# Issuing the first weight load ahead of SyncE's part in the entry barrier of a decode kernel

## The chip, the cores and the metric

The kernel runs on one core of one Trainium2 chip. The time is device microseconds of one execution, the median over several runs. A program can also run in a slower state. The "span" of a profile is counted from the first instruction that the trace shows (here SyncE's first one) to the last; the time is about 1.3 us longer than the span (654.95 and 653.6 in one run of the kernel before).

## The reference, cut to what matters

One decode step for two sequences: layer norm, grouped-query attention over a long cache, and a small gated MLP beside it.

```python
B, Sq, D = 2, 1, 512
Hq, Hkv, Sk, Dh = 32, 8, 32768, 128        # bf16 everywhere
xn = layernorm(x)
q  = xn @ wq                                # wq: 512 x 4096
p  = softmax(q @ k_cache^T * Dh**-0.5)      # k_cache: 2 x 8 x 32768 x 128
s  = (p @ v_cache) @ wo                     # wo: 4096 x 512
g  = silu(mlp(xn))                          # w3: 512 x 1792, w4: 1792 x 512
out = x + s * g
```

There are 16 (sequence, KV head) groups, each with 8 MiB of K and 8 MiB of V. Everything that has to be read comes to 280.5 MB; the output is 2 KB. The MLP's first branch (w1, w2) vanishes for a sequence of length one, and the kernel does not read it.

## The kernel before

The kernel has a static plan: SyncE issues nearly all loads on one DMA queue, in order, and waits only where a buffer has to come free first. The first load, wq, is recorded inside the framework's block; all other instructions are recorded after that block is closed.

```python
wq_t = kbuf[:, 2 * SLOT:3 * SLOT]
s_wq, s_out = nc.alloc_semaphore("s_wq"), nc.alloc_semaphore("s_out")
first = sp.dma_start(out=wq_t[:, 0:DK * HD], in_=A_wq.rearrange("(p k) f -> p (k f)", k=DK))
first.then_inc(s_wq, 16)
tc.no_tile_sem_insts.add(first.ins.name)

tc.close()
tc.compile()
# ... (semaphores)
k_w3 = d_w3.after(sp.dma_start(out=w34[:, 0:W4O], in_=...B_w3...), 16)
k_w4 = d_w4.after(sp.dma_start(out=w34[:, W4O:W4O + FK * D], in_=...B_w4...), 16)
# ... 
load_k(0)                                    # 8 MiB
load_half(A_v_cache, vbuf[:, :], s_v, 0, 1)  # 4 MiB

k_x0 = V(dve.memset(x_bf[:, :], 0.0))        # VectorE; then ScalarE loads x
wait(act, k_x0)
k_x = d_x.after(act.dma_start(out=x_bf[0:QP:BS, :], in_=A_x...), 16)
# ... layer norms, q = xn @ wq, the MLP: "the prologue" below
wait(sp, k_h2)
load_half(A_v_cache, vbuf[:, :], s_v, 0, 0)  # the first V group's other half, over w3 and w4
for m in range(1, NG):
    sp.wait_ge(p_k, m)                       # half of K group m-1 is used
    load_k(m)
    sp.wait_ge(p_o, m)                       # V group m-1 is used
    load_v(m)
# ... wo in seven parts, then the end:
k = V(dve.tensor_tensor(out=sg, in0=s_ps, in1=g4, op=ALU.mult))
k = V(dve.tensor_tensor(out=out4, in0=sg, in1=x4, op=ALU.add))
wait(sp, k)
sp.dma_start(out=out[:, 0, :].rearrange("b (n c) -> n b c", c=QW), in_=out4[0:QP:BS, :]).then_inc(s_out, 16)
sp.wait_ge(s_out, 16)
```

What the source does not show is how the built program starts. There is an entry block, in which every engine arrives at a barrier (GpSimd gathers the others, after it has set a few constants) and jumps. Then comes the framework's block, whose only work is the wq load, and which ends in another jump. Then come two more barriers, and only then the kernel's other instructions.

The softmax here doesn't subtract the row's maximum and nothing guards it: scores larger than these inputs give would overflow.

Of the kernel before, what the change touches and what calls it, by code (L numbers as in the profile page):

```python
# [43 lines left out]
def take(eng, sem, n=1):  # L44

    eng.wait_ge(sem, n).then_inc(sem, -n)  # L46


@with_exitstack
def kernel(  # L50
# [14 lines left out]
    nc = tc.nc  # L65
# [99 lines left out]
    first = sp.dma_start(out=wq_t[:, 0:DK * HD], in_=A_wq.rearrange("(p k) f -> p (k f)", k=DK))  # L165
# [2 lines left out]

    tc.close()
    tc.compile()  # L170

    d_x, d_w3, d_w4 = (Count(nc, n) for n in ("d_x", "d_w3", "d_w4"))
    s_k = [nc.alloc_semaphore(f"s_k{i}") for i in range(NPART)]
# [177 lines left out]
    for t in range(NQB):  # L351
        for k in range(DK):
            for n in range(NQ):
                c = (t * NQ + n) * GW
                i = pe.matmul(
                    sc[t][32 * n:32 * n + 32, :], lhsT=xT[:, k, :],
                    rhs=wq3[:, k, c:c + GW].rearrange("p (h w e) -> p h e w", h=rep * NB, e=2),
                    start=(k == 0), stop=(k == DK - 1), tile_position=(0, 32 * n),
                )
# [32 lines left out]
    for k in range(DK):  # L392
        for n in range(NQ):
            i = pe.matmul(
                h_ps[32 * n:32 * n + 32, 0:HW], lhsT=xT[:, DK + k, :], rhs=w3v[:, k, n * HW:(n + 1) * HW],
                start=(k == 0), stop=(k == DK - 1), tile_position=(0, 32 * n),
            )
# [29 lines left out]
    for f in range(FK):  # L427
        i = pe.matmul(h2[0:32, :], lhsT=h_bf[:, f, :], rhs=w4v[:, f, :], start=(f == 0), stop=(f == FK - 1))  # L428
# [27 lines left out]
    with act.Fori(0, NG) as m:  # L456
        for j in range(4):
            c = (NR - 1) * rep + 32 * j
            i = act.copy(  # L459
                out=z[32 * j:32 * j + 32, :, :, c:c + rep],  # L460
                in_=qr[32 * j:32 * j + 32, :, :, bass.ds(m * rep, rep)],
            )
        i.then_inc(s_z, 1)
        for i in range(NPART):
            take(act, s_sc)
            act.activation(  # L466
                out=eps_[i][:, :], in_=sc[i][:, :], func=ACT.Exp, scale=inv_sqrt_dh, accum_out=rss[i][:, :]
            ).then_inc(s_e, 1)
        take(act, s_o)
        act.copy(out=ob[:, :], in_=o[:, :]).then_inc(s_ob, 1)  # L470
# [4 lines left out]
    def then(inst):  # L475
        inst.then_inc(s_d, 1)
        take(dve, s_d)
# [52 lines left out]
    for j in range(NQ):  # L530
        n = B * NS if j < NQ - 1 else B * NS - 1
# [144 lines left out]
```

## Time and profile before

| | before |
|---|---|
| time, median of 6 runs | 654.96 us (654.88 to 655.34) |
| span of the profiled run | 654.2 us |
| share of the span that SyncE's queue filled | 99.2% of 16 DMA engines |
| TensorE, VectorE, ScalarE busy | 60%, 53%, 12% |
| wq issued, its first packet | 0.74 us, 1.76 us |
| last wo part landed | 651.47 us |

The page's slices of the kernel before, 40 equal ones over the span: the busy share of the 16 DMA engines in tenths and the bytes moved in GB/s. Below them is the first row of the table of DMA queues (queue, kind: packets, MB, share).

```profile
DMA  8999999999999999999999999999999999999997
GB/s 368 442 439 448 442 413 429 445 445 429 417 445 445 441 401 445 445 437 405 445 445 445 409 437 445 445 433 409 445 445 445 397 445 445 445 425 417 437 429 293
...
q1 hardware_dynamic: 6492, 280.50, 99.2%
```

Queue q1 is SyncE's. The DMA engines are full from the second slice to the last but one. A packet of 32768 B takes 1.213 us in the trace, which makes 16 x 32768 B / 1.213 us = 432 GB/s. Most of the bytes (243 MB) come in packets of 65536 B, which take 2.418 us each, or 434 GB/s on 16 engines. The scatter of the slices (397 to 448) I do not take for a changing rate: a packet is counted whole in the slice in which it starts, one slice of 16.4 us holds 6.8 rounds of 16 such packets, and counting 6 or 7 of them gives 385 or 449.

The start in time, the timeline of the kernel before (start us, duration us, engine, line, operation, out<-in; in brackets the idle time before it and what ended that). SPq is SyncE's own sequence, where the duration of a DMA is that of its issue only.

```profile
0.74 0.40 SPq L165 DMA_DIRECT2D kbuf<-in_A_wq_dram  x1
1.91 0.33 SPq L202 DMA_DIRECT2D vbuf<-in_B_w_dram  x1
1.92 0.20 POOL L238 MEMSET ident<- 128x128 bf16 x1 [1.47 <-POOLq L170]
2.04 0.27 DVE L230 MEMSET x_bf<- 128x256 uint32 x1 [2.04 <-PEq L170]
```

And who waited for whom at the start, the view of waits of SyncE's queue (total us, times, longest us), its last two rows:

```profile
SPq L660 <- PEq L660: 0.7, 1, 0.7
SPq L170 <- PEq L170: 0.4, 2, 0.3
```

SyncE has nothing to do in the entry block. It stands at the barrier for 0.7 us before the first byte of 280 MB has even been asked for. (The barrier is released by GpSimd, whose gather runs at 0.53 us; the view names the engine whose signal came last by the profile.)

The end, the chain of waits of the kernel before, its last rows (start us, duration us, what):

```profile
614.73 36.74 DMA kbuf<-in_A_wo_dram
651.47 0.04 issue
651.52 0.26 PE bank L614 x4
651.78 0.02 issue
651.80 0.30 DVE sg L638
652.10 0.02 issue
652.13 0.29 DVE out L640
```

The last wo part stood 36.74 us in the queue, then there are 0.26 us of matmuls, two VectorE operations and the store. Between the two ends, the trace shows how much was in the queue each time SyncE issued another load (bytes issued before, less the bytes of packets that had ended): never less than 3.1 MB, about 7 us of work. So the time is the start of the first packet, plus one unbroken stream, plus a tail.

### The profile page before, as it was taken

Reading aid. Unit: us, or ns where it says so; the run is one execution under the profiler, and the core shown is the slowest. Engines: PE = TensorE matmul, PEld = TensorE weight load, DVE = VectorE, ACT = ScalarE, POOL = GpSimd, SP = SyncE. Lnnn points to the kernel's source line nnn. Section 1 sums busy time; section 2 is a strip of 40 time slices with the busy share of each in tenths; the row PEclk is TensorE's granted clock in tenths of the full one; section 3 lists DMA queues with packets and bytes.
Section 4 is the critical chain, followed back from the end, with each engine's and each line's share of the span. In section 5 each row is a group of like instructions: output and inputs, shape, how many; then the busy total and the mean of one; then the engine's idle time right before and its main releaser. Section 6 shows DMA issues by size and latency. Waiting matters only on the chain. (4 is left out here: it accounts for less than half of the span.)

```text
span 654.2 us, 6541 instructions
## 1 busy us (share of the span) xinstructions
PE 390.2 (60%) x2406; PEld 156.8 (24%) x2438; DVE 345.7 (53%) x412; ACT 76.6 (12%) x184; POOL 7.7 (1%) x29
## 2 busy tenths in 40 slices
PE   0648285582838648293773829367283945828785
PEld 0222132230313212131231213123121322312322
DVE  4257092653909356291844719174480926539570
ACT  1320102010010200101020010201001020010100
POOL 3100000000000000000000000000000000000000
PEclk9769788696978868698786978878697896869798
DMA  8999999999999999999999999999999999999997
GB/s 368 442 439 448 442 413 429 445 445 429 417 445 445 441 401 445 445 437 405 445 445 445 409 437 445 445 433 409 445 445 445 397 445 445 445 425 417 437 429 293
DMA packets 6508, 280.56 MB, mean 429 GB/s; under 512 B 736, under 2 KB 1000, under 8 KB 1256
## 3 DMA queue, kind: packets, MB, share of 16 engines
q1 hardware_dynamic: 6492, 280.50, 99.2%
q8 instruction: 2, 0.03, 0.0%
q14 instruction: 2, 0.02, 0.0%
q10 hardware_dynamic: 12, 0.01, 0.0%
HBM read 280.50 MB, written 0.00 MB: 429 GB/s over the span
## 5 line engine op out<-in xcount | busy, mean ns | idle before, releaser
L562 PE MATMUL bank<-T,z 128*128 128x512 bf16 x992 | 271.6, 418 | 187.2 <-PEq L46 181.7
L489 DVE STREAM_TRANSPOSE T<-kbuf 128x1024 int32<-128x1024 int32 x256 | 290.5, 1206 | 127.2 <-DVEq L46 127.2
L562 PEld LDWEIGHTS bank<-T,z 128*128 128x128 bf16 x1024 | 96.0, 103 | 350.2 <-issue 274.4
L579 PE MATMUL bank<-vbuf,pt 128*16 128x512 bf16 x1024 | 75.6, 461 | 2.5 <-PEq L46 2.5
L466 ACT ACTIVATE ep<-bank 128x512 bf16<-128x512 f32 x32 | 19.1, 597 | 436.1 <-ACTq L46 436.1
L510 DVE RECIPROCAL rec<-bank 128x1 f32<-128x1 f32 (+1 forms) x17 | 2.9, 169 | 122.7 <-DVEq L46 122.7
L579 PEld LDWEIGHTS bank<-vbuf,pt 128*16 128x16 bf16 x1024 | 28.0, 104 | 41.9 <-issue 25.1
L498 DVE STREAM_TRANSPOSE pt<-ep 128x512 bf16<-128x512 bf16 x32 | 22.7, 708 | 22.0 <-DVEq L46 22.0
L544 PE MATMUL bank<-ob,sel_o 128*128 128x128 f32 x136 | 20.6, 298 | 16.4 <-PEq L46 16.4
L572 PE MATMUL bank<-ones_f,sm 128*128 128x1 f32 x32 | 6.6, 277 | 31.3 <-PEq L46 31.3
L544 PEld LDWEIGHTS bank<-ob,sel_o 128*128 128x128 f32 x136 | 17.7, 204 | 21.8 <-issue 21.8
L470 ACT COPY ob<-bank 128x512 f32<-128x512 f32 x16 | 9.4, 586 | 105.7 <-ACTq L46 105.7
L459 ACT ACT_TABLE_LOAD x16 | 20.5, 1283 | 0.3
L572 PEld LDWEIGHTS bank<-ones_f,sm 128*128 128x128 f32 x32 | 5.8, 225 | 32.2 <-issue 32.2
L459 ACT COPY z<-qr 32x16 bf16 x64 | 12.9, 201 | 0.7
L428 PE MATMUL bank<-vbuf,h_bf 128*32 128x512 bf16 x14 | 5.3, 565 | 5.7 <-DVE h_bf L425 5.7
L539 PE MATMUL bank<-ident 128*1 128x1 bf16 x64 | 8.4, 165 | 0.0
L305 PE MATMUL bank<-ident,xn_bf 17*128 17x17 bf16 x4 | 0.3, 179 | 13.4 <-POOL x L296 13.4
L539 PEld LDWEIGHTS bank<-ident 128*1 128x1 bf16 x64 | 4.0, 82 | 16.2 <-issue 14.4
L518 DVE TENSOR_REDUCE oA<-xm 128x128 f32 x16 | 5.9, 366 | 3.8 <-DVEq L46 3.8
L512 DVE SCALAR_TENSOR_TENSOR xm<-bank,rec,mask 128x128 f32<-128x128 f32 (+1 forms) x17 | 6.0, 351 | 2.5 <-DVEq L46 0.2
L466 ACT ACTIVATION_READ_ACCUMULATOR ep<-bank 128x1 f32 x32 | 6.4, 199 | 0.2
(75 smaller groups left out, 55.4 us busy)
## 6 DMA issues: line engine op xcount, KB each, us to landing
vbuf<-in_A_v_cache_dram SPq DMA_DIRECT2D x4, 4096.0 KB, 29.6
kbuf<-in_A_k_cache_dram SPq DMA_DIRECT2D x2, 4096.0 KB, 22.9
kbuf<-in_A_wq_dram SPq DMA_DIRECT2D x1, 4096.0 KB, 12.5
vbuf<-in_B_w_dram SPq DMA_DIRECT2D x2, 1792.0 KB, 17.4
kbuf<-in_A_wo_dram SPq DMA_DIRECT2D x3, 1024.0 KB, 34.4
kbuf<-in_A_wo_dram SPq DMA_DIRECT2D x1, 512.0 KB, 37.1
kbuf<-in_A_wo_dram SPq DMA_DIRECT2D x1, 256.0 KB, 37.3
kbuf<-in_A_wo_dram SPq DMA_DIRECT2D x2, 128.0 KB, 36.8
```

Source lines behind the costliest of these rows:

```text
L459: i = act.copy(out=z[32 * j:32 * j + 32, :, :, c:c + rep], in_=qr[32 * j:32 * j + 32, :, :, bass.ds(m * rep, rep)],)
L466: act.activation(out=eps_[i][:, :], in_=sc[i][:, :], func=ACT.Exp, scale=inv_sqrt_dh, accum_out=rss[i][:, :]).then_inc(s_e, 1)
L470: act.copy(out=ob[:, :], in_=o[:, :]).then_inc(s_ob, 1)
L489: dve.transpose(out=Ts[(NR * i + r) % T_BUFS][:, :].rearrange("p (b t k) -> p t b k", b=NB, t=RT), in_=kt[:, r * W:(r + 1) * W].rearrange( ...
L498: dve.transpose(out=pts[h][:, :, :].rearrange("p r (t h) -> p t r h", h=rep), in_=eps_[i][:, :].rearrange("p (t r h) -> p t r h", r=NR, h= ...
L512: dve.scalar_tensor_tensor(out=xm[p0:, :, :], in0=oT[p0:, :].rearrange("p (w r) -> p w r", w=WL), scalar=rec[p0:, 0:1], in1=mask[p0:, :].u ...
L518: dve.tensor_reduce(out=dst, in_=xm[p0:, :, :].rearrange("p w r -> p r w"), axis=AX.X, op=ALU.add).then_inc(s_r, 1)
L539: pe.matmul(mark_ps, lhsT=ident[:, 0:1], rhs=ident[:, 0:1], start=True, stop=True).then_inc(sem, 1)
L544: mm = pe.matmul(oT, lhsT=sel_o[:, t, :, :, :].rearrange("p j h w -> p (j h w)"), rhs=ob[:, t * Dh:(t + 1) * Dh], start=(t == 0), stop=(t ...
L562: mm = pe.matmul(sc[i][:, :], lhsT=z[:, nb, e, zc:zc + 128], rhs=Tb[:, nb, :, e], start=(r == 0 and nb == 0 and e == 0), stop=(r == NR - 1 ...
L572: pe.matmul(S, lhsT=sms[1][:, :], rhs=ones_f[:, 0:1], start=True, stop=True)
L579: mm = pe.matmul(o[32 * j:32 * j + VT * rep, :], lhsT=pts[h][:, r, a * VT * rep:(a + 1) * VT * rep], rhs=vt[:, u * VT:(u + 1) * VT, :].rea ...
```

## The change

Its intent is to issue the wq load as SyncE's very first instruction, ahead of SyncE's arrival at the entry barrier. It edits the built program: the load is taken out of its block and put in front of SyncE's first drain, which is the instruction that signals arrival.

```diff
+def begin(nc, ins):
+
+    blocks = nc.m.functions[0].blocks
+    for b in blocks:
+        b.instructions = [i for i in b.instructions if i.name != ins.name]
+    entry = blocks[0].instructions
+    at = next(n for n, i in enumerate(entry) if i.engine == ins.engine and isinstance(i, mybir.InstDrain))
+    blocks[0].instructions = entry[:at] + [ins] + entry[at:]
...
     tc.close()
     tc.compile()
+    begin(nc, first.ins)
```

In the built program the order of instructions shows one side effect. The framework's block, now empty of work, disappears, and with it one jump on every engine. Nothing else moves. (The profiles record no jumps, so no trace here shows this. ScalarE's next instruction comes 0.09 us after its release from the entry barrier in the kernel before, in the changed kernel and in e1 below alike.)

## The prediction

> **What bounds the kernel now.** The load stream. The line of DMA shares reads 9 (90% or more) in every slice but the first and last, and the queue table gives SyncE's queue 99.2% of 16 engines' span for 280.5 MB. Packets of 32768 B take 1.213 us each, so 16 engines move 16 x 32768 B / 1.213 us = 432 GB/s, and 280.5 MB need about 649 us of the 654.2 us span. Counting packets against SyncE's issues, the queue still holds at least 3.1 MB (7 us) at every load issue after the first, so it never runs dry; TensorE (60% busy) and VectorE (53%) hide under it. The chain of waits ends in the last wo load (36.74 us in the queue, landing at 651.47), 0.26 us of matmuls, two VectorE operations of 0.3 us, and the output store.
>
> The time is: start of the first packet (1.76 us), one unbroken stream, a tail of about 2.6 us. Only the first term can change.
>
> **What the change does.** In the timeline, SyncE arrives at the entry barrier at 0.00 us, is released at 0.65, and issues the wq load from 0.74 to 1.13; its first packet starts at 1.76, which is 1.03 us after the issue began and 0.63 after it ended. The Trainium skill ("DMA: Bandwidth & Descriptors", Specifications) gives about 0.6 us as first-byte latency on this path; the trace agrees. With the issue ahead of SyncE's arrival, it should begin at 0.00 and the first packet near 1.03: 0.7 us sooner. No operation is added, no byte moved; nothing else writes that buffer or semaphore before.
>
> The price is in the barrier. SyncE now arrives after its issue (0.40 us) and a gap, near 0.5 to 0.6 us. GpSimd, which gathers the barrier, is ready only at 0.53, so the release should move from 0.65 to about 0.70. (A drain behind the issue took 0.12 us: no wait for data.) In return the next barrier no longer waits for SyncE's issue: its gather was at 1.39 and should be near 0.95, and one block's jump is gone from every engine. The w3 issue should come near 1.4 instead of 1.91, the x load about 0.5 us sooner. None of that matters to the end: wq alone fills the queue for 9.7 us, and the prologue's own deadline (second half of the first V load, issued at 32.73) has 8.3 MB queued ahead.
>
> **How much is critical.** All of the 0.7 us: the stream has no gap in which a sooner start could be lost.
>
> **Predicted time:** 654.95 - 0.7 = 654.25 us, range 653.4 to 655.0; 0.11% faster. Chances: faster by over 2% 0.003, within 2% 0.994, slower by over 2% 0.003.
>
> **Right, if:** the wq issue opens the timeline at 0.00 and takes about 0.4 us; first release near 0.70; w3 issue near 1.4; wq lands 12.5 us after its issue; every later K and V issue comes about 0.7 us sooner; DMA share stays at 9; last wo landing near 650.8; tail unchanged.
>
> **Wrong, if:** the early issue takes longer, or its packets start later (a cold start that the barrier had hidden); the first packets, at 1.6 to 2.5 us rather than 1.2, get worse; or the measured time (1.3 us longer than the span) starts at some other event than SyncE's first instruction. The spread (0.46 us over three runs) is nearly as large as the effect, and another chip can shift both kernels.

## The result, and the profile after

| | before | after |
|---|---|---|
| time, median of 6 runs | 654.96 us | 654.20 us (654.05 to 654.49) |
| span of the profiled run | 654.2 us | 653.1 us |
| wq issued, its first packet | 0.74, 1.76 us | 0.00, 1.03 us |
| w3 issued | 1.91 us | 1.45 us |
| last wo part landed | 651.47 us | 650.42 us |

The ratio of the fast runs is 0.9988, with a 95% interval of 0.9975 to 1.0001. Ratios here are the mean time of one kernel's fast runs over that of the other's of the same rounds, so not quite the ratio of the medians quoted. By that interval alone the gain is not clear of noise; but all six runs of the changed kernel lie below all six of before (654.49 against 654.88).

The timeline of the changed kernel, its start, columns as above:

```profile
0.00 0.40 SPq L175 DMA_DIRECT2D kbuf<-in_A_wq_dram  x1
...
1.45 0.33 SPq L213 DMA_DIRECT2D vbuf<-in_B_w_dram  x1
1.45 0.20 POOL L249 MEMSET ident<- 128x128 bf16 x1 [1.02 <-POOLq L180]
1.58 0.27 DVE L241 MEMSET x_bf<- 128x256 uint32 x1 [1.58 <-PEq L180]
```

The waits of SyncE's queue in the changed kernel, its last three rows:

```profile
SPq L656 <- DMA out_dram<-out: 1.0, 1, 1.0
SPq L180 <- PEq L180: 0.5, 2, 0.3
SPq L671 <- PEq L671: 0.2, 1, 0.2
```

The issue takes 0.40 us as before and now lies where SyncE had stood idle: the wait at the entry barrier (last row) is down from 0.7 to 0.2 us. In the trace's semaphore instructions, the release comes at 0.72 us instead of 0.65, and GpSimd's gather of the next barrier at 0.93 instead of 1.39, since that one no longer waits for the issue. The zero of the time axis did not move with SyncE's new first instruction: the other engines arrive at the entry barrier at 0.13 (VectorE), 0.14 (ScalarE) and 0.32 us (TensorE's queue) in the kernel before and at 0.12, 0.13 and 0.31 us in the changed one.

The DMA slices of the changed kernel, and SyncE's queue:

```profile
DMA  9989999999999999999999999999999999999997
GB/s 386 482 388 448 447 446 402 441 441 446 405 441 441 446 401 446 441 446 397 450 441 446 401 446 441 450 425 417 450 441 429 413 450 441 446 397 444 420 446 297
...
q1 hardware_dynamic: 6492, 280.50, 99.4%
```

The chain of waits of the changed kernel, its end:

```profile
613.73 36.69 DMA kbuf<-in_A_wo_dram
650.42 0.04 issue
650.47 0.26 PE bank L625 x4
...
650.75 0.30 DVE sg L649
651.06 0.02 issue
651.08 0.29 DVE out L651
```

The end of the program is the same, only earlier. The two profiled runs differ by 1.1 us of span, more than the first packet moved (0.74 us). But the profiled run of before was the slow end of its kernel (its time was 655.52 us, above all six runs of the table), and its stream from first to last load packet took 649.43 us against 649.12. In the nine traces without a pause this length lies anywhere between 648.74 and 649.45 us, a scatter as large as the effect. So the medians are compared, not the two profiles.

### The profile page after: what moved, and what is told of

It is laid out like the page before. It is cut to its first block, busy times and chain, and to the rows that moved or that the text cites. A ratio compares the mean times of both kernels' runs of the same rounds, so it can differ in the third digit from the quotient of the medians.

```text
span 653.1 us, 6541 instructions
## 1 busy us (share of the span) xinstructions
PE 387.9 (59%) x2406; PEld 157.4 (24%) x2438; DVE 346.0 (53%) x412; ACT 76.6 (12%) x184; POOL 7.7 (1%) x29
## 5 line engine op out<-in xcount | busy, mean ns | idle before, releaser
L573 PEld LDWEIGHTS bank<-T,z 128*128 128x128 bf16 x1024 | 97.7, 103 | 350.9 <-issue 273.5
L590 PE MATMUL bank<-vbuf,pt 128*16 128x512 bf16 x1024 | 72.4, 444 | 4.5 <-PEq L46 3.3
## 6 DMA issues: line engine op xcount, KB each, us to landing
kbuf<-in_A_wq_dram SPq DMA_DIRECT2D x1, 4096.0 KB, 12.3
```

The source lines that it names most:

```text
L573: mm = pe.matmul(sc[i][:, :], lhsT=z[:, nb, e, zc:zc + 128], rhs=Tb[:, nb, :, e], start=(r == 0 and nb == 0 and e == 0), stop=(r == NR - 1 ...
L590: mm = pe.matmul(o[32 * j:32 * j + VT * rep, :], lhsT=pts[h][:, r, a * VT * rep:(a + 1) * VT * rep], rhs=vt[:, u * VT:(u + 1) * VT, :].rea ...
```

## The experiments

Theory: the end follows the first packet of the stream one to one, and nothing else of the change matters. The rivals are that the gain comes from the jump and block that are gone on every engine, or from the compute prologue, which also starts 0.46 us earlier, and that a shift at the start is partly absorbed by waits later on. All kernels are correct. "Against before" is the difference of the medians of the same chip and rounds.

| run | wq issued | first packet | VectorE starts | time, median (range) | against before |
|---|---|---|---|---|---|
| e0_after_again | 0.00 | 1.01 | 1.58 | 654.46 (654.34 to 654.83) | -0.53 |
| e1_behind_barrier | 0.74 | 1.76 | 2.04 | 655.04 (654.99 to 655.31) | +0.05 |
| e3a_after_barriers | 1.39 | 2.42 | 1.51 | 655.60 (655.53 to 655.77) | +0.61 |
| e3b_late_hops | 5.15 | 6.16 | 1.51 | 659.57 (659.23 to 659.71) | +4.58 |
| e2_three_ahead | 0.00 | 1.02 | 2.53 | 654.38 (654.16 to 654.80) | -0.72 |
| e4_prologue_late3 | 0.00 | 1.02 | 1.64 | 654.42 (654.17 to 654.84) | -0.68 |
| e5_prologue_late12 | 0.00 | 1.02 | 1.64 | 664.62 (663.99 to 666.38) | +9.52 |
| e6_store_split | 0.00 | 1.02 | 1.58 | 654.87 (654.62 to 655.12) | -0.23 |
| e7_late12_behind_x | 0.00 | 1.02 | 1.58 | 660.13 (658.29 to 661.88) | +4.95 |

The kernel before, in the rounds of these runs, had medians of 654.99 (first four), 655.10 (next four) and 655.18 (last), its first packet at 1.76 us and VectorE's start at 2.04 us.

### e0_after_again: the control

No edit: the changed kernel again.

> Control: the changed kernel again, on the same chip as the next three. Every theory expects what was measured: 654.2 us where the kernel before has 654.96, ratio 0.9988, first packet at 1.03 us.

It came out at -0.53 us, after -0.76 the first time. With e2 and e4 below, which also start the stream at 1.02 us, there are four measurements of the same start: -0.76, -0.53, -0.72 and -0.68, on average -0.67 us, where the first packet moved by -0.74. The highest of their 21 runs is 654.84 us, and the lowest of all runs of the kernel before 654.88.

### e1_behind_barrier: the missing block without the early issue

```diff
-    at = next(n for n, i in enumerate(entry) if i.engine == ins.engine and isinstance(i, mybir.InstDrain))
+    at = max(n for n, i in enumerate(entry)
+             if i.engine == ins.engine and isinstance(i, mybir.InstEventSemaphore)) + 1
```

> The wq load stays in the entry block (so its old block and that block's jump are gone, as in the change) but is issued behind SyncE's part in the barrier. Stream theory (the end follows the first packet one to one): issue near 0.69, first packet near 1.72 instead of 1.76, so 654.9 us, no gain over before. Rival (the gain is the missing block and jump on every engine): it keeps the whole gain, 654.2 us.

SyncE's first two issues stand where they stood in before, to 0.01 us:

```profile
0.74 0.39 SPq L175 DMA_DIRECT2D kbuf<-in_A_wq_dram  x1
1.91 0.33 SPq L213 DMA_DIRECT2D vbuf<-in_B_w_dram  x1
```

The time is that of before (+0.05 us). The missing block and jump are worth nothing that could be measured here.

### e3a_after_barriers: prologue early, stream late

```diff
-    begin(nc, first.ins)
+    # the load in the framework's block is taken out; behind the three barriers:
+    sp.dma_start(out=wq_t[:, 0:DK * HD], in_=A_wq...).then_inc(s_wq, 16)
     k_w3 = d_w3.after(sp.dma_start(...
```

> The wq load is issued behind all three barriers, directly ahead of the w3 load. The barriers then wait for no DMA issue, so the compute engines should start at about 1.3 us, as early as in the changed kernel or earlier, while the first packet comes later than in before: issue near 1.37, packet near 2.4. Stream theory: 0.6 us SLOWER than before, 655.6 us. Rival (the gain is the earlier start of the prologue on the compute engines): 0.5 us FASTER than before, 654.4 us.

This run pulls the two causes in opposite directions. VectorE started 0.53 us earlier than in before, and the first packet came 0.66 us later. The time rose by 0.61 us. It followed the packet, and the early prologue bought nothing.

```profile
1.39 0.39 SPq L209 DMA_DIRECT2D kbuf<-in_A_wq_dram  x1
1.39 0.20 POOL L248 MEMSET ident<- 128x128 bf16 x1 [0.95 <-POOLq L177]
1.51 0.27 DVE L240 MEMSET x_bf<- 128x256 uint32 x1 [1.51 <-PEq L177]
```

### e3b_late_hops: a dose clear of noise

```diff
+    s_hop = nc.alloc_semaphore("s_hop")
+    for _ in range(30):
+        sp.sem_inc(s_hop, 1)
+        take(sp, s_hop)
     sp.dma_start(out=wq_t[:, 0:DK * HD], in_=A_wq...).then_inc(s_wq, 16)
```

> As the kernel with the load behind all barriers, with 30 signal-and-wait pairs of SyncE with itself ahead of it, a larger dose clear of noise[...]. Stream theory: the time rises over before by what the first packet moved against 1.76 us, to within 0.3 us (some 3 to 5 us), and K and V issues later in the trace are all late by the same. Rival (a shift at the start is partly absorbed by waits later on): it rises by clearly less than the first packet moved. Rival of the compute prologue: no rise, since those engines are not held.

SyncE's issues in the timeline of e3b, the wq load and the second K load, and the same K load in the kernel before:

```profile
5.15 0.39 SPq L213 DMA_DIRECT2D kbuf<-in_A_wq_dram  x1
...
56.01 0.33 SPq L227 DMA_DIRECT2D kbuf<-in_A_k_cache_dram  x1
```

```profile
51.76 0.33 SPq L213 DMA_DIRECT2D kbuf<-in_A_k_cache_dram  x1
```

The 30 pairs moved the issue from 1.39 us (e3a) to 5.15, about 0.125 us each. The first packet came at 6.16 us, 4.40 us later than in before, and the time rose by 4.58 us. So a shift at the start is not absorbed anywhere: the difference of 0.18 us is within the 0.3 us set beforehand. The K issue that stood at 51.76 us in before stood at 56.01 here (+4.25). The next V issue went from 68.19 to 72.52 us (+4.33), the next K issue from 92.01 to 96.34 (+4.33). Not every issue followed: the first V group's other half, which waits for the compute prologue and not for the stream, was issued only 0.97 us later (33.70 against 32.73), with 9.4 MB still in the queue.

### e2_three_ahead: more loads ahead of the barrier

The edit is shown here against the changed kernel.

```diff
-def begin(nc, ins):
+def begin(nc, many):          # inserts all of them, in order
...
-    begin(nc, first.ins)
+    begin(nc, [first.ins, i_w3.ins, i_w4.ins])   # behind the recording of w3 and w4
```

> The changed kernel with the w3 and w4 loads too issued ahead of SyncE's part in the barrier. Stream theory: the first packet stays at 1.03 us and the stream was already full behind wq, so no further gain: 654.2 us, within 0.2 of the changed kernel, though the barrier is now released about 0.8 us later (near 1.55) and the whole compute prologue starts later. Rival of the compute prologue: about 0.8 us slower than the changed kernel, 655.0 us.

The three issues follow each other at 0.00, 0.45 and 0.91 us, and SyncE's arrival holds everybody up: VectorE starts at 2.53 us instead of 1.58:

```profile
2.53 0.27 DVE L241 MEMSET x_bf<- 128x256 uint32 x1 [2.53 <-PEq L180]
```

The time is that of the changed kernel (-0.72 us against before). So holding the barrier for 0.95 us costs nothing, and bringing further loads forward gains nothing: behind wq they only stand in the queue earlier.

### e4_prologue_late3 and e5_prologue_late12: how late may the prologue be?

```diff
+    for _ in range(6):           # 22 in e5
+        wait(dve, V(dve.memset(o[:, :], 0.0)))
     k_x0 = V(dve.memset(x_bf[:, :], 0.0))
```

> The changed kernel with six extra memsets on VectorE ahead of everything that engine does, each waiting for the one before, so that the x load and the compute prologue come about 3 us later; the loads of the stream's head are untouched. Stream theory: the queue held 7 to 17 us of work at every later issue, so nothing is lost: 654.2 us. Rival of the compute prologue: about 3 us slower, 657 us.

VectorE was held up for 4.0 us, the x load landed at 11.78 us instead of 9.27, and the first V group's other half was issued at 33.99 us instead of 32.34. The time did not change (-0.68 us).

> The same with 22 memsets, a delay of some 11 to 12 us. It tests whether the queue's stock is the slack that I take it for. The first group's scores start about 10 us later than at 41.26 us (the prologue had some 1.6 us to spare), so the second K load, issued at 50.9 us in the changed kernel with 8.3 us of work queued, is issued near 61 us, when the queue has been dry for 1 to 2 us; with the time to a new first packet (about 1 us) the stream should stand still once for 2 to 4 us: 656.2 to 658.2 us, far less than the delay of 11 to 12. If the prologue were on the critical path: some 11 us slower, 665 us. If the stock is larger than I count: no change.

This expectation missed: 656.2 to 658.2 us was expected and 664.62 measured. The trace shows why in two steps. First, the delay was far larger than planned. The memsets came every 0.667 us, 14.7 us in all, and the x load, issued at 16.55 us into the full stream, landed only at 27.58, 11.0 us later, where it took 7.4 us in the changed kernel. So the prologue came some 18 us late (its first cast at 27.94 us instead of 9.63, and the V half behind it 18.6 us late):

```profile
16.55 1.14 ACTq L246 DMA_DIRECT2D x_bf<-in_A_x_dram  x1
...
27.94 0.43 DVE L277 CAST T<-x_bf 128x512 f32<-128x512 bf16 x1 [10.22 <-DMA x_bf<-in_A_x_dram]
```

Second, with that delay the queue ran dry twice: from 49.53 to 51.87 us, where the V half was issued at 50.91 (the end of the first row below, which is merged), and from 63.19 to 69.93 us, where the second K load was issued at 68.97. SyncE's issues in the timeline of e5:

```profile
2.92 48.33 SPq L220 DMA_DIRECT2D vbuf<-in_A_v_cache_dram  x2
68.97 0.33 SPq L224 DMA_DIRECT2D kbuf<-in_A_k_cache_dram  x1
```

That makes 9.1 us without any packet. The mean idle time of the 16 engines between first and last load packet, which counts the ragged stop and start of each pause too, was 11.2 us against 0.4 in the changed kernel. The profiled run was the slowest of the four (666.38 us), 12.2 us above the profiled run of e4, which starts its stream alike and ran in the same rounds; by the medians the time rose by 10.2 us. So a delay of 18.6 us cost 10 to 12; the rest was covered by what stood in the queue.

### e7_late12_behind_x: the delay of e5 in the size that was meant

```diff
     wait(dve, k_x)
+    wait(dve, (v_, v_.n))
+    for _ in range(18):
+        wait(dve, V(dve.memset(o[:, :], 0.0)))
     k_xf = V(dve.tensor_copy(out=xf[:, :], in_=x_bf[:, :]))
```

> The delay of e5 came out at 18.6 us instead of 12, because 22 memsets took 14.7 us and the x load then took 11 us to land instead of 7; the queue stood dry twice. Here 18 such memsets (12.0 us at the 0.667 us from one to the next that e5 showed) stand behind the wait for x, so that the x load is not moved. Account of the stock: the second half of the first V load, issued at 32.3 in the changed kernel with 17.1 us queued (dry at 49.4), comes near 44.3, in time; it adds 9.5 us, so the queue is dry at 58.9; the second K load follows it by 18.1 us, as in e5, at 62.4, and its first packet 1.0 us later, so the stream stands still once for about 4.5 us: 654.4 + 4.5 = 658.9 us, between 658.0 and 659.8. If the miss of e5 lay in the account rather than in the size of the delay: 12 us slower, 666 us, or no change.

The DMA slices of e7 show the one pause as a dip in the fourth slice:

```profile
DMA  9997999999989999999999999999999998999997
GB/s 387 472 410 292 443 446 394 438 446 442 446 390 442 446 442 446 410 422 446 442 446 438 394 446 446 442 446 426 406 446 446 442 446 386 446 446 412 444 432 305
```

SyncE's issues in the timeline of e7 (a merged row runs from its first issue to the end of its last; the first V group's other half is the end of the second row shown):

```profile
2.35 0.45 SPq L224 DMA_DIRECT2D kbuf<-in_A_k_cache_dram  x1
2.91 42.16 SPq L220 DMA_DIRECT2D vbuf<-in_A_v_cache_dram  x2
62.80 0.33 SPq L224 DMA_DIRECT2D kbuf<-in_A_k_cache_dram  x1
```

The V half was issued at 44.74 us (44.3 expected), with 2.1 MB still in the queue. The K load came at 62.80 us (62.4), and the queue was dry once, from 59.59 to 63.76 us, 4.2 us (4.5). The account by stock names the right pause at the right place. The time was 660.13 us, 0.3 us above the expected band (658.0 to 659.8), and its four runs scatter over 3.6 us; those of e5 scatter over 2.4, those of the kernels without a pause over 0.2 to 0.7. The ragged stop and start of the pause, which I had not counted, adds about 0.8 us to it: the mean idle time of the engines rose by 5.0 us (5.4 against 0.4), not 4.2. That is 0.5 us more than the 4.5 us counted, of an excess of 1.2 us over the 658.9 us expected. What the scatter comes from once the compute chain sets a pause was not tried and stays open.

### e6_store_split: the other end of the sum

```diff
-    wait(sp, k)
-    sp.dma_start(out=out[:, 0, :].rearrange("b (n c) -> n b c", c=QW), in_=out4[0:QP:BS, :]).then_inc(s_out, 16)
-    sp.wait_ge(s_out, 16)
+    for b, eng in enumerate((sp, act)):
+        wait(eng, k)
+        eng.dma_start(out=out[b, 0, :]..., in_=out4[b * BS:...:32, :]).then_inc(s_out, 16)
+    sp.wait_ge(s_out, 16 * B)
```

> The changed kernel with the output store split in two, one half issued by SyncE and one by ScalarE at the same time. The one store took 0.70 us to issue and landed 1.0 us after that; a simpler shape took 0.33 us at other places. The tail is the only other term of the sum: start of the first packet + stream + tail. Stream theory: what the issue gets shorter is gained whole, up to 0.35 us: 653.9 us. If ScalarE's issue is slow (its x load took 1.14 us to issue) it is lost instead: up to 0.4 us slower, 654.6 us.

Neither engine got much faster at issuing (timeline of e6, last rows):

```profile
651.55 0.64 SPq L654 DMA_DIRECT2D out_dram<-out  x1
651.56 0.56 ACTq L654 DMA_DIRECT2D out_dram<-out  x1
```

and the wait for the store to land became longer (waits of SyncE's queue in e6; the changed kernel has 1.0, shown above):

```profile
SPq L657 <- DMA out_dram<-out: 1.3, 1, 1.3
```

ScalarE's packets started 0.65 us after its issue ended, but SyncE's 0.92 us after its own (the single store's start 0.59 to 0.60 us after it in all other traces): the two did not start side by side. In the profiles, the tail from the store's issue to SyncE's last wait grew from 1.73 to 1.99 us. The time is 0.45 us above that of e4, which ran in the same rounds with the single store (654.87 against 654.42). That is outside what was expected, 653.9 to at worst 654.6. The cost I had feared, a slow issue on ScalarE, is not what happened; the longer way from issue to landing is, and it accounts for 0.26 us of the 0.45, with the rest within the scatter of the runs. So a longer tail came out as a longer time, and this edit is not the one to shorten it. No experiment pointed to a version better than the changed kernel.

## Why the prediction was right

- **The bound.** It was right that one unbroken stream bounds the kernel. The shares of the DMA engines before and after, and the dose of e3b (+4.58 us for +4.40), show it.
- **The early issue.** Predicted at 0.00 us with its first packet near 1.03; measured at 0.00 and 1.03. The fear of a cold start that the barrier had hidden was unfounded: the issue took 0.40 us, the packet followed 0.63 us behind its end, and the first 16 packets took 1.83 us on average against 1.84 in before.
- **The first-byte latency.** The Trainium skill ("DMA: Bandwidth & Descriptors", Specifications) gives about 0.6 us on this path. The traces agree if one counts from the end of the issue, which the page does not say: 0.62 to 0.63 us from there to the first packet, both at 0.00 and at 5.15 us (e3b). From the start of the issue it is 1.03 us.
- **The barrier.** The release was predicted near 0.70 and came at 0.72; the next gather was predicted near 0.95 and came at 0.93; w3 was predicted near 1.4 and came at 1.45 us. That none of it matters was only argued then; e1, e2, e3a and e4 show it.
- **The size.** 0.7 us and 654.25 us were predicted; 0.76 us and 654.20 were measured. The four measurements of this start average 0.67 us. That the median met the prediction to 0.05 us is luck, since the four medians lie between 654.20 and 654.46 us. The stated range (653.4 to 655.0) also held the time of the kernel before, so the number alone would not have told the effect from none; the experiments did.
- **A detail that did not hold.** "Every later K and V issue comes about 0.7 us sooner" is true of most K issues (14 of the 16 after the first came 0.6 to 0.9 us sooner: 50.93 against 51.76, 91.31 against 92.01, 169.20 against 169.84) and not of the V issues: 68.96 against 68.19 is later, 105.63 against 108.52 is 2.9 us sooner. A V issue waits for TensorE, not for the stream, and its time varied from trace to trace by more than the effect. It costs nothing because the queue still holds over 4 MB then.
- **The last landing** was predicted near 650.8 and came at 650.42; the profile of before had been a slow run, as told above. wq landed 12.3 us after its issue (12.5 predicted), and the tail from the last landing to the end of the span was 2.72 us against 2.73 before.

## What to carry to other kernels

Where a profile shows one resource full from its first use to its last, the time is "start of that use, the use, the tail", and only what moves its first or its last instant counts. Ask whether anything stands in front of the first load that does not guard it, such as a program's own barriers. A barrier may be held up in exchange, as long as what it delays has stock to live on; count that stock in the queue at each later issue, since e5 shows that it is large here but not endless.

## What the Trainium skill lacked or had wrong

- "DMA: Bandwidth & Descriptors" (Issuing engines are not separate DMA queues) says that initiating DMAs on several engines at once saves the sequencer's time to initiate. In e6 two halves issued at the same instant saved little (0.64 and 0.56 us against 0.69 for the whole) and SyncE's half then started 0.92 us after its issue instead of about 0.6, so the whole was slower by some 0.3 us. The page lacks that of two stores issued at once one can start later than a single one; this one trace shows it, and its cause was not tried.
- The same page (Queues, rings and completion order) describes a round-robin between queues, but no page says how long a small load on a second queue waits behind a full stream. The 8 KB x load landed 1.6 us after the start of its issue with no stream running (e3b), 7.4 us after it at the start of the stream, and 11.0 us in the middle of it (e5). There its packets came in four strands, and those of one strand stood 2.46 us apart, about one of the stream's packets of that time (65536 B, 2.418 us); in the changed kernel they stood 1.25 us apart, beside packets of 32768 B that take 1.213 us. Both fit a turn of one packet each.
- The same page (Where 436 GB/s comes from) has two limits, about 358 GB/s for HBM to one core and 435 GB/s for the fabric, and says that for transfers from HBM the first binds. For one core alone it does not hold here: it read 432 GB/s from HBM (16 packets of 32768 B in 1.213 us), just under the second. The page's own measurement with one core (425 GB/s), which it calls near the fabric's rate, shows the same; no run here had two cores streaming.
- No page says what the barriers inside a program's start cost; the figures of "Runtime: NRT & Kernel Launch" are for the barriers that the runtime puts around a program. Here the last of three of them released SyncE at 1.84 us, with the issue between them, and at 1.38 us with the issue in front.
